# A decode step of attention plus GLU: TensorE's program rolled into a loop of seven turns over five heads, inside a hinted loop of two turns

## The chip, the core and the metric

The kernel runs on one core of a Trainium2 chip. The metric is device microseconds of one execution; the number given for the kernel before is the median of three runs. The profile is one execution, recorded by the hardware profiler.

## The reference

One decode step for a batch of two: a layer norm, then in parallel an attention over the last 2048 positions of a cache and a bilinear GLU, all added to the input. Everything is float32.

```python
B, D, Hq, Sk, Dh, F = 2, 512, 32, 8192, 128, 1376
xn = layernorm(x)                                  # x: [B, 1, D]
W = min(4096, max(256, Sk // 4))                   # 2048
q = (xn @ wq).reshape(B, 1, Hq, Dh)
k, v = k_cache[:, :, Sk - W:, :], v_cache[:, :, Sk - W:, :]     # [B, Hq, W, Dh]
p = softmax(einsum("bhqd,bhkd->bhqk", q, k) * Dh ** -0.5)
o = einsum("bhqk,bhkd->bhqd", p, v).reshape(B, 1, Hq * Dh)
h = (xn @ w_gate) * (xn @ w_up)
out = x + o @ wo + h @ w_down
```

Each head of each of the two sequences has its own keys and values, so each is used once: 134 MB of cache and 25 MB of weights are read for one result of 2 x 512.

## The kernel before, in words

The host lays all inputs out as one stream of blocks in the order in which the kernel needs them (`laid_out`, `blocks`). SyncE (SP) loads the blocks in that order into three slots of SBUF of 31 x 512 columns on 128 partitions; a load is issued when a slot is free, that is when every field of the block in it has been used (`pump`, `done`, lines 297 to 323). A head's keys are one field of 4096 columns: on each partition 16 positions of both sequences (line 746). Its values may be cut into pieces of 512 columns and spread over blocks (`vp` fields).

For each head, in order:

- `products`, `sums` (lines 432 to 443): VectorE (DVE) multiplies the keys by the query, which stands in PSUM, copied to all 128 partitions, and sums over the 128 elements of a position. Each is one instruction over 128 x 4096.
- `maxima`, `weights` (lines 445 to 466): DVE takes the largest score of each partition, GpSimd (POOL) the largest over the partitions, ScalarE (ACT) scales it and takes the exponentials, one instruction for each sequence, into p; POOL sums over the partitions, and DVE takes the reciprocal (`reciprocals`).
- `weigh` (line 484): TensorE (PE) multiplies p with the values, eight calls a head, into one of two banks `o_ps`. `copy_out` (line 494): ACT copies the bank to `o_sb`. `transpose` (line 501): PE brings the result to columns, ACT scales it into `oT`. `project_o` (line 520): PE multiplies by the head's part of `wo` and adds to `acc`.

The query projection is cut into a piece per head (`project_q`, two calls for each head into four heads' query in PSUM). The GLU is worked in the first blocks (`project_gu`, `gate`, `down`). The last heads are written out by hand (lines 659 to 720): for these, results are accumulated in a form spread over partitions (`accumulate`, four calls of 128 columns), and TensorE is given matmuls without use (`keep_busy`) between its steps.

All engines' instructions are recorded into one list in program order by `Flow.add` (line 162). `emit` (line 184) then finds which waits are needed and writes each engine's instructions, in the order of that list, with semaphore waits between the engines. So each engine runs strictly in the order of the program text, and all profile rows carry line 243, from which `emit` writes them; SP's waits are at line 242. A call of `pe.matmul` in float32 becomes two pairs of a weight load and a matmul.

Of the kernel before, what the change touches and what calls it, by code (L numbers as in the profile page):

```python
# [14 lines left out]
P = 128  # L15
B, D, H, DH, SK, F = 2, 512, 32, 128, 8192, 1376
W = min(4096, max(256, SK // 4))
J = W // P
# [6 lines left out]
LAG = 3  # L25
# [5 lines left out]
HG = 4  # L31
GC = HG * DH
JG = J // 4
CK, CQ, CO = B * J * DH, NC * GC, D
CP = CQ // NC
UNIT = CK + max(CP, CO)
STEP = 31 * FB
NP = 6
NV = CK // FB
KS = [3, 1, 2, 1, 2, 2, 1, 2, 2, 2, 1, 2, 2, 2, 1, 2, 2, 1]  # L40
WD = [(0, 2), (2, 4), (4, 7), (7, NFC - 1), (NFC - 1, NFC)]
NS = 3
BUFS = 3
BASE = 30 * 1024
FX = FR // NS

# [10 lines left out]
def blocks():  # L57

    def wd(n):
        return [("wd", i, D) for i in range(*WD[n])]

    def k(h):
        return [("k", h, CK)] + ([("wq", h, CP)] if h + HG < H else [])  # L70

    def v(h):
        return [("v", h, CK), ("wo", h, CO)]

    def gu(half):
        n = NC * (FH[half][1] - FH[half][0])
        return [("wg", half, n), ("wu", half, n)]

    ones = [("pick", 0, 8 * B), ("rows", 0, NFB * B)]
    first = [("x", 0, B * NC)] + ones + [("w", 0, NC * DH)]  # L80
    ahead = [[("w", 1, CQ - NC * DH)], gu(0) + gu(1), [("wr", 0, NS * P)] + wd(0)]
    pieces = [(h, n) for h in range(H - 1 - LAG) for n in range(NV + 1)]
    loads, h = [], 0
    for i, n in enumerate(KS):
        fields = (ahead[i] if i < len(ahead) else []) + sum((k(h + j) for j in range(n)), [])
        h += n
        room = (STEP - sum(w for _, _, w in fields)) // FB if i > 1 else 0
        taken, pieces = pieces[:room], pieces[room:]
        for g in sorted({g for g, _ in taken}):
            assert g < h - n  # L90
            ns = [m for t, m in taken if t == g]
            parts = [m for m in ns if m < NV]
            if parts:
                p0, p1 = parts[0], parts[-1] + 1
                fields.append(("vp", (g, p0, p1), FB * (p1 - p0)))
            if ns[-1] == NV:
                fields.append(("wo", g, CO))
        assert not pieces or pieces[0][0] >= h - NP
        loads.append(fields)
    assert not pieces and h == H - 1  # L100
    loads += [k(H - 1) + v(H - 1 - LAG) + wd(1)]
    out = [(("f", 0), first)] + [(("s", i), fields) for i, fields in enumerate(loads)]
    late, last = ("s", len(loads)), ("s", len(loads) + 1)
    out += [(late, v(H - 3)), (late, v(H - 2)), (last, [("v", H - 1, CK)])]
    out += [(last, [("wo", H - 1, CO)] + wd(2))]
    return out + [(last, wd(n)) for n in range(3, len(WD))]


class Flow:
# [7 lines left out]
    def __init__(self, nc):  # L117
        self.nc = nc
        self.units = {
            "pe": nc.tensor, "dve": nc.vector, "act": nc.scalar, "pl": nc.gpsimd, "sp": nc.sync,  # L120
        }
        self.ops, self.seen, self.free = [], {}, {}
        self.low = -(-nc.sbuf_base // 32) * 32
# [38 lines left out]
    def add(self, unit, make, writes, reads):  # L162
        n = len(self.ops)
        deps = set()
        for aps, write in ((reads, False), (writes, True)):
            for ap in aps:
                if not isinstance(ap.tensor, (bass.SBTensorHandle, bass.PSumTensorHandle)):
                    continue
                name, p0, p1, f0, f1 = self.box(ap)
                kept = []  # L170
                for old in self.seen.get(name, []):
                    m, w, a0, a1, b0, b1 = old
                    if m != n and (write or w) and a0 < p1 and p0 < a1 and b0 < f1 and f0 < b1:
                        deps.add((m, w))
                        if write and p0 <= a0 and a1 <= p1 and f0 <= b0 and b1 <= f1:
                            continue
                    kept.append(old)
                self.seen[name] = kept + [(n, write, p0, p1, f0, f1)]
        self.ops.append((unit, make, deps))
# [3 lines left out]

    def emit(self):
        nc, ops = self.nc, self.ops
        place, count = [], {}
        for n, (unit, make, deps) in enumerate(ops):
            key = ("dma", n) if make[0] == "dma_start" else unit
            count[key] = count.get(key, 0) + 1
            place.append((key, count[key]))  # L190
        knows = [None] * len(ops)
        known = {unit: {} for unit in self.units}
        waits = []
        for n, (unit, make, deps) in enumerate(ops):
            have = known[unit]
            need = {}
            for m, wrote in deps:
                key, at = place[m]
                if key == unit and (unit == "pe" or unit in ("dve", "act") and not wrote):
# [8 lines left out]
            ]  # L208
            for m in keep:
# [11 lines left out]
        told = {m for keep in waits for m in keep} | {len(ops) - 1}  # L221
        sems, value, at = {}, {}, {}
        order = sorted({place[m][0] for m in told}, key=lambda key: (key in ("dve", place[-1][0]), str(key)))
        if order[-1] != place[-1][0]:
            order.append(order.pop(-2))
        for key in order:
            sems[key] = nc.alloc_semaphore("done_" + (key if isinstance(key, str) else f"load{key[1]}"))
# [7 lines left out]
        for n, (unit, (method, args, kwargs), _) in enumerate(ops):  # L235
            eng = self.units[unit]
            keep = sorted(
                waits[n], key=lambda m: (isinstance(place[m][0], tuple) and m >= landed, m)
            )
            landed = max([landed] + [m for m in keep if isinstance(place[m][0], tuple)])  # L240
# [8 lines left out]
            if n == len(ops) - 2:  # L249
                assert unit == "dve"  # L250
                nc.vector.sem_clear(range(nums[0], nums[-2]))
        assert unit == "sp"
# [19 lines left out]
def sliding_attention_plus_glu_kernel(  # L272
# [13 lines left out]
    ]  # L286


    todo, at = [], 0
    for key, fields in blocks():  # L290
        todo.append((key, fields, at))
        at += P * pitch(fields)
    tiles, used, left, got = {}, {}, {}, {}
    for key, fields, _ in todo:
        left[key] = left.get(key, 0) + len(fields)

    def pump():
        while todo:
            key, fields, at = todo[0]
            if key not in tiles:  # L300
                if key[0] == "f":
                    n = sum(w for _, _, w in fields)
                    tiles[key] = flow.tile([P, n], "first")
                elif not slots:
                    return
                else:
                    tiles[key] = slots.pop(0)
                used[key] = 0
            todo.pop(0)
            c0 = used[key]  # L310
            for kind, i, w in fields:
                got[kind, i] = (tiles[key][:, used[key] : used[key] + w], key)
                used[key] += w
            c1 = used[key]
            src = stream[at : at + P * pitch(fields)].rearrange("(p i) -> p i", p=P)
            sp.dma_start(tiles[key][:, c0:c1], src[:, : c1 - c0])

    def done(kind, i):
        _, key = got.pop((kind, i))
        left[key] -= 1  # L320
        if left[key] == 0 and key[0] != "f":
            slots.append(tiles.pop(key))
            pump()

    pump()
    xT = got["x", 0][0].rearrange("p (b c) -> p b c", b=B)
    pick = got["pick", 0][0].rearrange("p (r s b) -> p r s b", s=2, b=B)
    rows = got["rows", 0][0]
# [22 lines left out]
    p_ring = [flow.tile([P, B, JG, 8 * B], f"p{i}") for i in range(NP)]  # L351
# [4 lines left out]
    oT_ring = [flow.tile([P, M], f"oT{i}") for i in range(4)]  # L356
    for t in oT_ring:
        pl.memset(t, 0.0)
# [21 lines left out]
    xnb = flow.tile([P, NC * B, P], "xnb")  # L380
    dve.tensor_copy(
        xnb, xn.rearrange("p c b -> p (c b)").unsqueeze(2).to_broadcast([P, NC * B, P])
    )

    q_ps, s_t, mm_t, p_t, sum_t, rec_t, o_sbs, oT = {}, {}, {}, {}, {}, {}, {}, {}
    n_acc = bank = 0

    q_banks = [flow.bank([P, B, GC], f"q{i}") for i in range(2)]

    def q_bank():  # L390
        q_banks.append(q_banks.pop(0))
        return q_banks[-1]

    def side(h):

        return int(h % 3 == 0)

    q_first = tr[:, P : 3 * P].rearrange("p (b n) -> p b n", b=B)

    def project_first(i):  # L400
        w = got["w", i][0].rearrange("p (c n) -> p c n", c=NC)
        if i == 0:
            q = q_first
        else:
            q_ps[0] = q_bank()
            q = q_ps[0][:, :, DH:]
        for b in range(B):
            for c in range(NC):
                pe.matmul(
                    q[:, b, :], xnb[:, c * B + b, :], w[:, c, :],  # L410
                    start=(c == 0), stop=(c == NC - 1),
# [410 lines left out]
```

## Time and profile before

| what | value |
|---|---|
| median of 3 runs | 376.09 us (375.97 to 376.46) |
| the profiled execution | span 374.6 us, from its first to its last instruction |
| instructions | 2741, of which 1094 matmuls and 1094 weight loads |
| busy | PE 66%, DVE 79%, ACT 16%, POOL 7% of the span |
| DMA | 159.70 MB, 426 GB/s over the span |
| packets of instructions | 8 of 16 KB on one queue, 4 of 8 KB on another |
| mean granted clock of TensorE | 0.813 |

Rows of the timeline read: start in us, length in us, engine, line, operation, output <- inputs, how many instructions were merged into the row, and in brackets the idle time before it with what ended it. Rows of the chain of waits read: start, length, what. The slices of the page cut the span in 40 parts of 9.37 us. "PEld" is TensorE's weight load, which overlaps its matmuls; "step" are the three slots.

### The profile page before, as it was taken

How to read it: one execution, taken by the hardware profiler on the slowest of the kernel's cores; microseconds unless marked ns; L12 is line 12 of the kernel's file. 1: busy time of each engine (PE TensorE's matmuls, PEld its weight loads, DVE VectorE, ACT ScalarE, POOL GpSimd, SP SyncE). 2: the span in 40 equal slices, each digit the busy share in tenths (PEclk: the TensorE clock that was granted, in tenths of full speed). 3: DMA queues.
4: the chain of work that ended last, by engine and by line, in shares of the span. 5: the costliest groups of instructions: out<-in, count | busy, mean ns of one | idle time of the engine just before them, and what ended most of it. 6: DMA issues, size and time to landing. Idle time of an engine off the chain costs nothing.

```text
span 374.6 us, 2741 instructions
## 1 busy us (share of the span) xinstructions
PE 248.4 (66%) x1094; PEld 86.8 (23%) x1094; DVE 295.1 (79%) x147; ACT 58.1 (16%) x259; POOL 25.3 (7%) x78
## 2 busy tenths in 40 slices
PE   3167675896578157855658585781488647476997
PEld 3033124231132013211212121320122112111344
DVE  3069998994599994599999945999999459999760
ACT  1002012111022012110202020300121201111232
POOL 1000000100001000000000000010001000000010
PEclk9759695898689758896969886998689868666999
DMA  8999999999999999999999999999999999999996
GB/s 345 420 465 454 450 432 435 434 434 424 427 427 434 434 434 434 436 434 441 434 435 429 434 434 434 434 429 434 434 435 434 429 434 434 428 426 416 414 432 250
DMA packets 3950, 159.70 MB, mean 426 GB/s; under 512 B 466, under 2 KB 610, under 8 KB 994
## 3 DMA queue, kind: packets, MB, share of 16 engines
q1 hardware_dynamic: 3938, 159.54, 98.6%
q8 instruction: 8, 0.13, 0.1%
q14 instruction: 4, 0.03, 0.0%
HBM read 159.47 MB, written 0.07 MB: 426 GB/s over the span
## 4 chain that ended last, share of the span: by engine, by line
DMA 64%; DVE 26%; PE 7%; ACT 1%; issue 0%; SPq 0%
DMA step<-in_stream_dram 64%; DVE s L243 13%; DVE step L243 13%; PE q L243 3%; PE acc L243 2%; PE o_ps L243 2%; PE tr L243 1%; ACT o_sb L243 0%; DVE m L243 0%; ACT oT L243 0%; DVE rec L243 0%; SPq L243 0%; DVE o_out L243 0%
## 5 line engine op out<-in xcount | busy, mean ns | idle before, releaser
L243 DVE TENSOR_TENSOR step<-step,q 128x4096 f32<-128x4096 f32 x31 | 136.8, 4411 | 47.0 <-DMA step<-in_stream_dram 47.0
L243 DVE TENSOR_REDUCE s<-step 128x32 f32<-128x4096 f32 x32 | 141.4, 4419 | 1.1
L243 PE MATMUL q<-step,xnb 128*128 128x512 f32 (+1 forms) x128 | 79.0, 759 | 80.5 <-DMA step<-in_stream_dram 80.5
L243 PE MATMUL o_ps<-step,p 128*16 128x512 f32 (+1 forms) x512 | 98.5, 730 | 11.2 <-DMA step<-in_stream_dram 11.2
L243 PEld LDWEIGHTS q<-step,xnb 128*128 128x128 f32 x128 | 28.0, 238 | 123.5 <-DMA step<-in_stream_dram 92.9
L243 PE MATMUL acc<-step,oT 128*9 128x512 f32 (+1 forms) x88 | 39.1, 604 | 8.7 <-ACT oT L243 8.7
L243 PE MATMUL tr<-first,o_sb 128*128 128x2 f32 (+2 forms) x198 | 29.1, 266 | 17.9 <-ACT o_sb L243 12.0
L243 PEld LDWEIGHTS tr<-first,o_sb 128*128 128x128 f32 x198 | 26.8, 205 | 40.6 <-ACT o_sb L243 31.3
L243 PEld LDWEIGHTS o_ps<-step,p 128*16 128x16 f32 x512 | 17.6, 107 | 78.6 <-issue 64.9
L243 ACT COPY o_sb<-o_ps 128x512 f32<-128x512 f32 (+1 forms) x24 | 13.8, 576 | 121.4 <-PE o_ps L243 121.4
L243 POOL PARTITION_ALL_REDUCE mm<-m x32 | 11.3, 355 | 268.6 <-DVE m L243 258.7
L243 ACT ACTIVATE nm<-mm 128x2 f32<-128x2 f32 x32 | 6.5, 203 | 148.0 <-POOL mm L243 148.0
L243 ACT ACTIVATE p<-s,nm 128x16 f32<-128x16 f32 x64 | 19.2, 300 | 1.0
L243 POOL PARTITION_ALL_REDUCE sum<-rs x32 | 12.7, 398 | 69.1 <-ACT p L243 69.1
L243 ACT ACTIVATE oT<-tr,rec 128x1 f32<-128x1 f32 x64 | 12.2, 260 | 27.0 <-PE tr L243 27.0
L243 DVE TENSOR_TENSOR step<-step,tr 128x4096 f32<-128x4096 f32 x1 | 4.4, 4422 | 14.8 <-DMA step<-in_stream_dram 14.8
L243 ACT ACTIVATION_READ_ACCUMULATOR p<-s,nm 128x1 f32 x64 | 11.9, 187 | 0.0
L243 PE MATMUL o_ps<-step,xn 128*2 128x512 f32 (+1 forms) x48 | 10.1, 548 | 0.0
L243 PEld LDWEIGHTS acc<-step,oT 128*9 128x9 f32 x88 | 4.6, 94 | 21.1 <-ACT oT L243 14.5
L243 DVE TENSOR_TENSOR o_out<-acc,x_nat 128x128 f32<-128x128 f32 x1 | 0.3, 292 | 8.4 <-PE acc L243 8.4
L243 DVE TENSOR_REDUCE m<-s 128x2 f32<-128x32 f32 x32 | 6.0, 186 | 1.1
L243 DVE RECIPROCAL rec<-sum 128x2 f32<-128x2 f32 x32 | 5.0, 155 | 1.9 <-POOL sum L243 1.9
(43 smaller groups left out, 41.5 us busy)
## 6 DMA issues: line engine op xcount, KB each, us to landing
step<-in_stream_dram SPq DMA_DIRECT2D x14, 7936.0 KB, 37.7
step<-in_stream_dram SPq DMA_DIRECT2D x2, 7680.0 KB, 32.0
step<-in_stream_dram SPq DMA_DIRECT2D x1, 7872.0 KB, 58.2
step<-in_stream_dram SPq DMA_DIRECT2D x1, 7808.0 KB, 38.8
step<-in_stream_dram SPq DMA_DIRECT2D x1, 4864.0 KB, 30.3
step<-in_stream_dram SPq DMA_DIRECT2D x2, 2304.0 KB, 19.6
step<-in_stream_dram SPq DMA_DIRECT2D x1, 2048.0 KB, 18.3
step<-in_stream_dram SPq DMA_DIRECT2D x1, 1024.0 KB, 19.8
```

Source lines behind the costliest of these rows:

```text
L243: made = getattr(eng, method)(*args, **kwargs)
```

## The change

TensorE's program is no longer written out head by head. The heads after the first three are taken in six turns of five, T = 6, G = 5; a seventh turn runs one of the sections alone. The body is written once, and for that every turn must address the same places, so the layout is made periodic:

- The keys and values of a head are laid out with one sequence on each half of the partitions (PB = 64), 32 positions each, still 128 x 4096. The query of a head is one row that differs between the halves; `project_q` makes the queries of five heads at once (eight calls, into PSUM) and ACT copies them to SBUF (`q_sb`). The maximum is taken by two DVE instructions, one on each half.
- A block has a fixed slot, and a slot may be loaded in part: a load is issued when the columns that it overwrites are no longer live. A turn has three blocks, with the keys of two, two and one heads, and the values of the five heads that are three behind.
- p, `oT`, `rec` and others are rings of five. The results of heads 0 and 1 of a turn share one bank (`SPLIT`), those of heads 2, 3 and 4 the other.
- PE's waits inside the loop are on token semaphores that hold the same value in each turn: another engine adds a token when its work is done, PE takes it off. A load's landing is told by SP, which waits for it (`tell`) and then adds the token.
- Of the GLU's last product two chunks stay early, one (`HOLE`) is moved behind the loop, its weights in a gap of the last query weights, and seven are accumulated at the end. `keep_busy` is gone.

The loop itself, and the loop of two turns around all of TensorE's program:

```python
TWICE = ("pe",)

    @contextlib.contextmanager
    def twice(self, unit):
        if unit not in TWICE:
            yield
            return
        eng = self.units[unit]
        with self.nc.Fori(0, 2, engines=(eng.engine,), hint_back_edge=True) as turn:
            with eng.If(turn > 0):
                yield
...
            # in emit, for PE: body has sections "q", "a", "b"; turns is 6, 7, 6
            with nc.tensor.Fori(0, max(turns.values())) as turn:
                for section, ns in body.items():
                    short = turns[section] < max(turns.values())
                    with nc.tensor.If(turn < turns[section]) if short else contextlib.nullcontext():
                        for n in ns:
                            write(n)
...
            if part:
                for key in sorted(points[part[0], part[2]]):
                    eng.wait_ge(sems["token", key], 1).then_inc(sems["token", key], -1)
```

The blocks of the stream (slot, first column, fields), with `vp(h, p0, p1)` a part of a head's values:

```python
    out.append((1, 0, k(*range(AHEAD))))                       # AHEAD = 3
    out.append((2, 0, [("wq", 0, CQ)] + gu + [("wr", 0, NS * P)] + wd(range(NE))))
    k0, v0 = AHEAD, 0
    for t in range(T):
        last = t == T - 1
        out.append((0, 0, k(k0, k0 + 1) + vp(v0) + vp(v0 + 1, 0, VA)))        # VA = 5
        out.append((1, 0, k(k0 + 2, k0 + 3) + vp(v0 + 1, VA) + vp(v0 + 2) + vp(v0 + 3, 0, VB)))
        b, c = vp(v0 + 3, VB), vp(v0 + 4)                                     # VB = 1
        if not last:
            out.append((2, 0, [("wq", t + 1, CQ)] + k(k0 + 4) + b + c))
        else:
            at = CQ + CK
            out += [(2, at, b), (2, at + sum(w for _, _, w in b), c)]
        k0, v0 = k0 + G, v0 + G
    # then: values of head 30, of head 31 in two parts, wo of 31 with four chunks
    # of w_down, two chunks, one chunk
```

And the order of the program, which is each engine's order:

```python
    def part_a(t):
        with flow.loop("a", t):
            weigh(G * t, 0, NV)
            weigh(G * t + 1, 0, VA)

    def post(t, group):
        d = transpose(group, copy_out(group))
        scale_out(group, d)
        for n in SPLIT[group]:
            project_o(G * t + n)

    def part_b(t):
        with flow.loop("b", t):
            weigh(G * t + 1, VA, NV)
            post(t, 0)
            weigh(G * t + 2, 0, NV)
            weigh(G * t + 3, 0, VB)

    def part_c(t):
        with flow.loop("b", t):
            weigh(G * t + 3, VB, NV)
            weigh(G * t + 4, 0, NV)
            post(t, 1)

    for t in range(T):
        part_q(t)
        h = AHEAD + G * t
        scores(h, lambda: part_a(t))         # scores: products, sums, then(),
        scores(h + 1)                        #         maxima, weights, reciprocals
        scores(h + 2, lambda: part_b(t))
        scores(h + 3)
        if h + 4 < H:
            scores(h + 4, lambda: part_c(t))
        else:
            reciprocals(h + 3)
            part_c(t)
    part_a(T)

    down(HOLE)
    acc_sb = flow.tile([M, D], "acc_sb")
    dve.tensor_copy(acc_sb, acc)
    weigh(H - 1, VA, NV)
    o_sb = copy_out(0)
    accumulate(carry, acc_sb)
    d = transpose(0, o_sb)
    n = len(SPLIT[0])
    dve.tensor_tensor(oT[:, :n, ::RB], d, rec[:, :n, :], op=ALU.mult)
    chunks = [c for group in TAIL for c in group]
    for c in chunks[:3]:
        down(c)
    project_o(H - 2)
    project_o(H - 1)
    for c in chunks[3:]:
        down(c)
```

More of the change, by code (lines that the diff above doesn't have):

```diff
@@ L1 @@
+import contextlib
 import math
@@ L57, in blocks @@
 def blocks():
[L66 to L106, printed above, removed]
+    def k(*heads):
+        return [("k", h, CK) for h in heads]
+    def vp(h, p0=0, p1=NV):
+        return [("vp", (h, p0, p1), FB * (p1 - p0))] + ([("wo", h, CO)] if p1 == NV else [])
@@ L394, in side @@
[L394 to L408, printed above, removed]
+    xnb = xnb.rearrange("p (c b) n -> p c (b n)", b=B)
+    s_t, mm_t, sum_t = {}, {}, {}
+    q_ps = flow.bank([P, 4 * FB // 2], "q")
@@ L479, in accumulate, with weigh @@
         n_acc += 1
-    def keep_busy(n):
-        pe.matmul(spare[:, 0:n], mean_w, spare_in[:, 0:n], start=True, stop=True)
-    def weigh(h, v, parts, first, last):
-        for n, part in enumerate(parts):
-            b, i = divmod(part, JG)
+    def weigh(h, p0, p1):
+        group = next(n for n, g in enumerate(SPLIT) if h % G in g)
+        heads = SPLIT[group]
+        v = got["vp", (h, p0, p1)]
+        cols = 4 * B * len(heads)
+        for n in range(p0, p1):
+            k, i = divmod(n, 4)
@@ L675, in sliding_attention_plus_glu_kernel, with scores @@
-    transpose([H - 6, H - 5], o_sbs[1])
-    for g in (H - 7, H - 6, H - 5):
-        project_o(g)
-    keep_busy(256)
-    maxima(h)
-    reciprocals(h - 1)
-    products(h + 1)
-    o_sb = pv([HF])
-    down(1)
+    def scores(h, then=None):
+        products(h)
+        sums(h)
+        if then:
+            then()
+        maxima(h)
+        weights(h)
+        if h >= 1:
+            reciprocals(h - 1)
+    project_first()
+    for h in range(AHEAD):
+        scores(h)
+    for half in range(2):
+        project_gu(half)
@@ new lines, in sliding_attention_plus_glu_kernel, with part_q @@
+    gate()
+    for c in range(NE):
+        down(c)
+    down_rest()
+    def part_q(t):
+        with flow.loop("q", t):
+            project_q(t)
+    def part_a(t):
[13 more added lines that the diff above has]
+            weigh(G * t + 3, 0, VB)
```

546 lines of the change are left out of this document (279 added, 267 removed).

## The prediction

> **What bounds the kernel now.** I read the page first: span, slices, queues.
>
> ```profile
> span 374.6 us, 2741 instructions
> PE 248.4 (66%) x1094; PEld 86.8 (23%) x1094; DVE 295.1 (79%) x147; ACT 58.1 (16%) x259; POOL 25.3 (7%) x78
> DMA  8999999999999999999999999999999999999996
> GB/s 345 420 465 454 450 432 435 434 434 424 427 427 434 434 434 434 436 434 441 434 435 429 434 434 434 434 429 434 434 435 434 429 434 434 428 426 416 414 432 250
> q1 hardware_dynamic: 3938, 159.54, 98.6%
> q8 instruction: 8, 0.13, 0.1%
> DMA 64%; DVE 26%; PE 7%; ACT 1%; issue 0%; SPq 0%
> step<-in_stream_dram SPq DMA_DIRECT2D x14, 7936.0 KB, 37.7
> ```
>
> The 16 DMA engines are full from the first slice to the last, at 434 GB/s, and 159.5 MB must come in: the body of the kernel is the stream. A block of 7,936 KB needs 18.7 us of that rate and lands 37.7 us after its issue, so a whole block still stands ahead of it in the queue when it is issued: the releases of the buffers have that much to spare. Only the head and the tail can move the time, and whatever slows the stream itself. Then the chain of waits, its last pieces, and the timeline of the last 20 us:
>
> ```profile
> 340.49 0.19 DVE m L243
> 340.68 0.07 DVE rec L243
> 340.75 4.33 DVE step L243
> 345.08 0.02 issue
> 345.10 4.43 DVE s L243
> 349.53 0.02 issue
> 349.55 18.29 DMA step<-in_stream_dram
> 367.84 0.04 issue
> 367.89 1.06 PE o_ps L243 x16
> ```
>
> ```profile
> 21.98 4.42 DVE L243 TENSOR_TENSOR step<-step,tr 128x4096 f32<-128x4096 f32 x1 [14.81 <-DMA step<-in_stream_dram]
> ...
> 352.07 4.42 DVE L243 TENSOR_TENSOR step<-step,q 128x4096 f32<-128x4096 f32 x1 [2.26 <-DMA step<-in_stream_dram]
> ...
> 357.01 4.40 DVE L243 TENSOR_REDUCE s<-step 128x32 f32<-128x4096 f32 x1
> ...
> 361.44 0.19 DVE L243 TENSOR_REDUCE m<-s 128x2 f32<-128x32 f32 x1
> ...
> 361.72 0.35 POOL L243 PARTITION_ALL_REDUCE mm<-m  x1 [2.62 <-DVE rec L243]
> ...
> 362.70 0.29 ACT L243 ACTIVATE p<-s,nm 128x16 f32<-128x16 f32 x1
> ...
> 372.26 0.12 PEld L243 LDWEIGHTS acc<-step,hT 128*9 128x9 f32 x8 [0.22 <-DMA step<-in_stream_dram]
> 372.74 0.29 DVE L243 TENSOR_TENSOR o_out<-acc,x_nat 128x128 f32<-128x128 f32 x1 [8.38 <-PE acc L243]
> 373.05 0.35 SPq L243 DMA_DIRECT2D out_dram<-o_out  x1
> ```
>
> The last load lands at 372.2, TensorE ends at 372.7, 0.5 us behind it, and the output takes 1.9 more to 374.6. The last head's keys land at 352.07 (20 us ahead of the stream's end), its sums end at 361.4, its weights p are ready at 363.0, and TensorE then waits for values until 367.8. So the softmax of the last head has 4.8 us to spare. This tail is what the change rebuilds. The time shown, 376.09, is 1.5 us above the profiled span of 374.6; I work on the span and add that 1.5 at the end. About 0.2% (0.75 us) can be told from no change.
>
> **The change, part by part.** *Bytes.* Caches and weights are the same; only the order and the placing in the three slots differ. Blocks of 30x512 columns (7,864 KB decimal, 18.1 us at 434 GB/s) follow one another: per turn two blocks with two heads' keys each and one with a single head's keys. Nothing for the sum.
>
> *DVE.* Products and sums keep their shape (128x4096), so a head costs what the chain shows from one m (340.49) to the point after the next sums (349.55): 9.06 us. The maximum becomes two reduces on half the partitions, at most another 0.19. Five heads take 46 us of a turn of 54.4: hidden behind the stream, with 8 us to spare per turn. The releases: slot 0 of the next turn needs the projection of the turn's first two heads (second block's landing plus some 6 us), slot 1 that of the third head (third block's landing plus some 11 us), both due 18 us after those landings, when the block ahead has landed. I price mid-stream gaps at nothing; if a release came 8 us later than this, they would cost what is over.
>
> *TensorE's program.* What a loop can save is the fetching of its instructions: 8 packets, 0.13 MB, so 16 KB each. At 0.1% of 16 engines' 374.6 us they hold 6 us of engine time (3 to 9 by the rounding), 0.4 to 1.1 each, and a load ends with its slowest engine. If the loop fetches nothing, the stream ends between 0 and 1.1 us earlier; I take 0.4, since fetches at the start and end stay and the other engines' do too. The two-turn wrapper costs a jump over the program and back, before the first load has landed: nothing, unless it takes longer than the 15 us that DVE waits for the first keys.
>
> *Tokens.* SP now also waits on a load and then tells TensorE, so its DMA issues queue behind these waits; in program order each issue needs consumers of the same or a later load, so none is held back by one. Nothing, to some tenths of a us per hand-over.
>
> *The tail.* This is the term that counts. In the sixth turn the keys of heads 30 and 31 lie in the second block. Call its landing B. Behind it come 2,097 + 2,359 + 2,359 + 1,311 + 786 + 1,311 + 524 + 262 KB = 11.01 MB, 25.4 us at 434 GB/s. The stream's end, 372.2 less 0.4 = 371.8, puts B at 346.4. From there, in us after B:
>
> DVE still owes 0.3 of the block before (two heads, 18.4 with the additional maxima, against 18.1 per block), then two heads: sums of head 31 end at 18.6. From sums to p took 361.41 to 362.99 before, 1.6: p of head 31 is ready at 20.2, 5.2 ahead of the stream's end; before it was 9.2 ahead.
>
> What stands behind it is the point. The sixth turn has no fifth head, so `part_c(5)` is written after `scores(31)`. ScalarE runs in program order: its copy of the bank for heads 27 to 29 stands behind the exponentials of head 31, which wait for DVE until 18.8. TensorE has the values of 28 and 29 at 4.8 and 10.3 and is through with them at 12, then stands at the transposes until the copy comes, and everything later stands behind: three projections, then all of heads 30 and 31. The rows that price it:
>
> ```profile
> 340.61 6.37 PE L243 MATMUL o_ps<-step,p 128*16 128x512 f32 x38 [5.31 <-DMA step<-in_stream_dram]
> ...
> 344.00 0.17 PEld L243 LDWEIGHTS o_ps<-step,p 128*16 128x16 f32 x4 [0.68 <-issue]
> ...
> 345.10 0.11 PEld L243 LDWEIGHTS o_ps<-step,p 128*16 128x16 f32 x4 [0.32 <-issue]
> ...
> 349.45 2.74 PE L243 MATMUL acc<-step,oT 128*9 128x512 f32 x6
> ...
> 358.07 1.90 PE L243 MATMUL o_ps<-step,p 128*16 128x512 f32 x16
> ...
> 360.04 0.59 ACT L243 COPY o_sb<-o_ps 128x512 f32<-128x512 f32 x1 [1.43 <-PE o_ps L243]
> 360.68 1.05 PEld L243 LDWEIGHTS tr<-first,o_sb 128*128 128x128 f32 x8 [0.48 <-ACT o_sb L243]
> ...
> 361.85 0.41 ACT L243 ACTIVATE oT<-tr,rec 128x1 f32<-128x1 f32 x2 [1.23 <-PE tr L243]
> ...
> 370.83 0.84 PE L243 MATMUL acc<-step,hT 128*9 128x128 f32 x24
> ```
>
> ```profile
> 135.15 3.78 PE q L243 x4
> ```
>
> ```profile
> 3.76 0.58 PE L243 MATMUL tr<-st,mean_w 128*128 128x2 f32 x2 [3.76 <-DVE st L243]
> ```
>
> The two weight-load rows show how the pace changes: four loads every 0.85 us (0.17 busy, 0.68 idle) up to 344.0, every 0.43 from 345.1, so TensorE needs some 4 us of work after its pause to come up to speed.
>
> Step by step, fast end and slow end: copy 0.65 (20.8); transposes, 8 instructions, 1.1 (or 2.3 at the 0.29 each that the first matmuls show) to 21.9 or 23.1; the first scaled pair 0.45; three projections, 6 instructions, 2.7 (or 4.6, at 0.95 each as in the q row until TensorE has run for some 4 us) to 25.1 or 28.2; weighing head 30, 16 instructions, 1.9; the first five pieces of head 31, 1.2; leaving the loop, of which no row of this trace has a price, 0.2, taken from short gaps between instructions and bounded by 0 and by 2 us for a fetch (below); the moved chunk in 512 columns, 2 instructions at 0.46, 0.9; three pieces, 0.7; copy with its hand-overs 0.8; transposes 1.1; three accumulations (24 instructions) 0.84, two projections 0.56, four accumulations 1.1. Sum: 34.4 or 37.4. TensorE ends at 346.4 + 34.4 = 380.8 or 383.8, that is 9 to 12 behind the last landing where it was 0.5. The idle stretch from 12 to 20.8 is longer than the 5.31 in the row above, after which 38 instructions took 6.37 (0.17 each) where 16 in a dense stretch took 1.90 (0.12 each), so the chain's start is slow; its later part is dense. I take 36.0: TensorE ends at 382.4, the span at 384.3, the time at 385.8.
>
> [...]
>
> **Rivals.** [...]
>
> [...]
>
> *Faster by the fetches alone.* Place: the last landing. If ScalarE's order does not hold TensorE, since head 31's scores are there early, only the slowest DMA engine counts: it ends up to 1.1 earlier, 375.0 to 376.0. It decides from the point where p of head 31 stands 14 us ahead of the stream's end; by the rows it is 5.2. Against it is that DVE needs 18.4 us for two heads that land 25.4 ahead of the end.
>
> *In between.* The copy gets past (an order other than I read), but p at 20.2 still leads: five pieces 1.2 or 2.1, 0.2, 0.9, 0.7, 0.8, 1.1, 2.5: 27.6 to 29.5, TensorE ends 374.0 to 375.9, the time 377.4 to 379.3.
>
> **How the numbers follow.** Tail chain as worked out 0.66 (384.2 to 387.2 between its ends); with more fetching 0.16 (388.5 to 391); in between 0.08; faster 0.07; a remainder of 0.03 within 0.2%. All but the last two are slower: 0.90, same 0.03, faster 0.07. The range takes the first case whole and nearly all of the second, and reaches below the first for hand-overs mis-sized by 2 us or more: 381.5 to 390.5. Left out are the faster, same and in-between cases (0.18) and the far end of the second (0.02).
>
> **What would show it.** In the profile after: the last stream landing within 1 us of 372.2; the last k landing near 346 and the last sums ending near 365; then on ScalarE the copy of the bank right behind the last exponentials; TensorE idle for some 8 us ahead of the transposes of heads 27 to 29; the chain ending in PE and ACT pieces of 14 to 17 us, and DMA slices that fall to nothing about 12 us before the span's end. [...] I am wrong if DMA is busy up to the last 3 us, or if mid-stream slices fall below 420 GB/s.

## The result, and the profile after

The changed kernel takes 408.9 us (median of 4 runs, 407.92 to 409.72) against 376.05 us before (375.97 to 376.46): 1.0869 times as long, with an interval of 1.0851 to 1.0887. It is slower, as predicted, but by 32.9 us where 9.7 were forecast, and 18 us beyond the range. The page of the changed kernel, cut to the lines that answer to those of before, with one group of instructions (columns: count, busy time, mean ns of one, idle time ahead of them with its releaser):

```profile
span 408.4 us, 2613 instructions
...
DMA  8998999985999999999989999999999999996491
GB/s 365 426 464 386 475 392 475 391 385 193 428 421 398 463 403 373 397 404 463 409 367 433 409 409 457 409 367 445 380 427 451 403 397 403 415 403 292 186 415 49
...
q1 hardware_dynamic: 4226, 159.54, 92.5%
q8 instruction: 2, 0.03, 0.0%
...
L330 POOL PARTITION_ALL_REDUCE mm<-m x32 | 109.9, 3434 | 227.5 <-DVE m L330 227.5
```

The same bytes came in, but the stream no longer runs through. Slice 10 moved 193 GB/s, slices 37 and 38 292 and 186, and the middle averages less than the 434 of before. TensorE's instruction packets fell from 8 to 2. The line that nobody asked for is the last one. GpSimd's maximum over the partitions is the same instruction as before, on the same operands, and the group of before has it at a tenth of the time:

```profile
L243 POOL PARTITION_ALL_REDUCE mm<-m x32 | 11.3, 355 | 268.6 <-DVE m L243 258.7 <-DVE rec L243 9.9
```

VectorE's waits in the changed kernel (columns: waited for, total us, times, longest) say that the stream is not what it waits for. Before, its one large wait was the landing of keys, 61.9 us in 17 times. Now:

```profile
DVE step L330 <- ACT q_sb L330: 35.8, 3, 15.5
DVE step L330 <- ACT first L330: 29.8, 3, 10.5
DVE step L330 <- DMA step<-in_stream_dram: 10.2, 1, 10.2
```

`q_sb` and `first` are the two buffers into which ScalarE copies the queries of a turn. So once in each of the six turns the products wait for their queries. The timeline of the changed kernel shows one whole turn of that, with the start of the first turn ahead of it (start, length, engine, instruction, idle time before it; "SPq" is SyncE's queue, and its row here is the load of the second turn's first block):

```profile
67.20 4.43 DVE L330 TENSOR_TENSOR step<-step,q_sb 128x4096 f32<-128x4096 f32 x1 [15.54 <-ACT q_sb L330]
...
96.94 0.33 SPq L330 DMA_DIRECT2D step<-in_stream_dram  x1
...
181.84 4.43 DVE L330 TENSOR_TENSOR step<-step,q_sb 128x4096 f32<-128x4096 f32 x1 [10.24 <-ACT q_sb L330]
...
219.37 4.64 POOL L330 PARTITION_ALL_REDUCE mm<-m  x1 [3.15 <-DVE m L330]
219.39 4.41 DVE L330 TENSOR_TENSOR step<-step,q_sb 128x4096 f32<-128x4096 f32 x1
224.04 0.20 ACT L330 ACTIVATE nm<-mm 128x2 f32<-128x2 f32 x1 [8.31 <-POOL mm L330]
225.13 0.58 ACT L330 COPY o_sb<-o_ps 128x512 f32<-128x512 f32 x1
225.86 1.84 PE L330 MATMUL tr<-first,o_sb 128*128 128x6 f32 x8 [6.94 <-PEq L322]
228.30 4.18 PE L330 MATMUL acc<-step,oT 128*9 128x512 f32 x6 [0.59 <-PEq L322]
228.75 0.35 POOL L330 PARTITION_ALL_REDUCE mm<-m  x1 [3.15 <-DVE m L330]
232.41 4.59 PE L330 MATMUL q<-step,xnb 128*128 128x512 f32 x16
237.03 0.69 ACT L330 COPY first<-q 128x640 f32<-128x640 f32 x1 [6.83 <-PE q L330]
237.83 4.43 DVE L330 TENSOR_TENSOR step<-step,first 128x4096 f32<-128x4096 f32 x1 [8.97 <-ACT first L330]
...
352.30 4.42 DVE L330 TENSOR_TENSOR step<-step,first 128x4096 f32<-128x4096 f32 x1 [10.46 <-ACT first L330]
```

Two things are to be read here. First, the all-reduce at 219.37 starts with the fifth head's product and ends with it (223.8 and 224.0). The one at 228.75 has no product beside it and takes 0.35. Secondly, the rows close a ring. VectorE takes four heads (37.5 us from 181.84 to 219.37), GpSimd's maximum of the fourth stands beside the fifth product (4.7), ScalarE takes the exponentials (1.1) and only then, in its order, copies the bank (0.7); TensorE transposes (2.4 with ScalarE's scaling), projects three heads (4.1) and makes the next turn's queries (4.6); ScalarE copies these (0.8); and VectorE may begin the next turn. The sum is 56.0, which is 237.83 less 181.84. From the first turn's product at 67.20 to the sixth's at 352.30 there are five turns of 57.0 us on average; the one shown is the shortest. The stream needs 54.4 for a turn, so the ring sets the pace, slots come free late, and the stream dries. All of TensorE's idle time that this leaves is put down to its sequencer (PEq), which stands at a token: over the run 62.6 us ahead of the weighings, 100.3 ahead of the transposes, 7.1 ahead of the projections. TensorE's pace enters the ring too: its granted clock is 0.50 from 221 to 231 us, and its transposes and projections, 6.6 us here, take 4.2 in the tail, where it is 1.00; by these rows the low clock is worth some 2.3 us of the ring, an estimate that no run tested.

The first standstill comes before the ring has closed once. The first turn's queries are made behind the products of the GLU, so its first product began at 67.20, although its keys had landed at 56.3. The load of the second turn's first block waits for results of this turn; it was issued at 96.94, when the block ahead of it had landed at 92.7, and the stream stood still from 92.4 to 97.9 us (slice 10). No run made these first queries earlier.

The tail of the changed kernel, in the same columns, has the order that the prediction described:

```profile
387.12 3.63 PE L330 MATMUL o_ps<-step,p 128*24 128x512 f32 x30 [0.21 <-PEq L322]
...
390.88 0.32 ACT L330 ACTIVATE p<-s,nm 64x32 f32<-64x32 f32 x1
...
391.31 0.58 ACT L330 COPY o_sb<-o_ps 128x512 f32<-128x512 f32 x1
...
392.04 1.03 PE L330 MATMUL tr<-first,o_sb 128*128 128x6 f32 x8 [1.29 <-PEq L322]
...
403.87 1.06 PE L330 MATMUL acc<-step,hT 128*9 128x128 f32 x32
```

ScalarE's copy stands right behind the last exponentials, and TensorE ends 13.7 us after them. But here the order costs little: the bank itself is full only at 390.75, half a microsecond before the exponentials end, and TensorE stands for 1.29 us ahead of its transposes, where some 8 were forecast.

### The profile page after: what moved, and what is told of

It reads as the page before. It is cut to its first block, busy times and chain, and to the rows that moved or that the text cites. A ratio compares the mean times of both kernels' runs of the same rounds, so it can differ in the third digit from the quotient of the medians.

```text
span 408.4 us, 2613 instructions
## 1 busy us (share of the span) xinstructions
PE 200.2 (49%) x940; PEld 73.6 (18%) x940; DVE 302.5 (74%) x179; ACT 59.5 (15%) x250; POOL 124.2 (30%) x84
## 5 line engine op out<-in xcount | busy, mean ns | idle before, releaser
L330 POOL PARTITION_ALL_REDUCE mm<-m x32 | 109.9, 3434 | 227.5 <-DVE m L330 227.5
L330 PE MATMUL o_ps<-step,p 128*24 128x512 f32 (+1 forms) x512 | 82.3, 670 | 62.6 <-PEq L322 62.6
L330 DVE TENSOR_TENSOR step<-step,q_sb 128x4096 f32<-128x4096 f32 x15 | 66.1, 4409 | 35.8 <-ACT q_sb L330 35.8
L330 DVE TENSOR_TENSOR step<-step,first 128x4096 f32<-128x4096 f32 x14 | 61.7, 4409 | 29.8 <-ACT first L330 29.8
L330 PE MATMUL tr<-first,o_sb 128*128 128x6 f32 (+1 forms) x118 | 25.8, 337 | 102.6 <-PEq L322 100.3
L330 PEld LDWEIGHTS o_ps<-step,p 128*24 128x24 f32 (+1 forms) x512 | 19.0, 104 | 110.1 <-issue 108.1
L330 PE MATMUL q<-step,xnb 128*128 128x512 f32 (+1 forms) x96 | 28.1, 446 | 0.0
L330 ACT ACTIVATE p<-s,nm 64x32 f32<-64x32 f32 x64 | 20.4, 319 | 1.4
L330 PEld LDWEIGHTS q<-step,xnb 128*128 128x128 f32 x96 | 15.3, 195 | 19.3 <-issue 19.3
L330 DVE TENSOR_REDUCE m<-s 64x1 f32<-64x32 f32 x64 | 11.5, 180 | 1.5
L330 ACT ACTIVATION_READ_ACCUMULATOR p<-s,nm 64x1 f32 x64 | 11.8, 185 | 0.0
L330 PEld LDWEIGHTS o_ps<-step,xn 128*2 128x2 f32 x48 | 2.8, 95 | 32.9 <-DMA step<-in_stream_dram 23.6
## 6 DMA issues: line engine op xcount, KB each, us to landing
step<-in_stream_dram SPq DMA_DIRECT2D x17, 7680.0 KB, 23.8
```

The source lines that it names most:

```text
L330: made = getattr(eng, method)(*args, **kwargs)
```

## The experiments

The theory after the result: GpSimd's maximum is held up while VectorE multiplies two operands from SBUF (4.64 us beside the product at 219.39, 0.35 at 228.75); that makes the ring longer than a turn of the stream; the tail order costs what was predicted; the wrapper costs little. The rival: the loop's branches refetch instructions, or the wrapper's hint does, and TensorE is late for that reason. Times are medians, each beside runs of the kernel before on the same chip (376.04, 376.29 and 375.99 in the three groups of runs).

### Queries read from PSUM

```diff
-        act.copy(q_sb[t % 2], q_ps[:, :GC])
...
-        q = ... q_sb[t % 2][:, n * DH : (n + 1) * DH]
+        q = ... q_ps[:, n * DH : (n + 1) * DH]
```

> The queries are read from PSUM by the products, as before, and the copy to SBUF is gone; nothing else differs. Theory (the all-reduce of GpSimd is held up while VectorE multiplies two SBUF operands, and its 4.64 us lie on a ring VectorE - GpSimd - ScalarE - TensorE - VectorE that closes once per turn): the all-reduce of m is back at 0.35 us in every head, a turn goes from 57.0 to the stream's 54.4 us or the ring's 52, the profile loses 20 us or more: 384 to 390 us. Rival (the loop itself, its branches, tokens and a TensorE that is cold sets the turn): the turn stays at 56 to 57 us, the time within 3 us of 408.9.

Measured: 392.09 us (390.92 to 392.93), 1.0431 times before (1.0414 to 1.0448), 16.8 below the changed kernel and just above the 384 to 390 expected. The group of the all-reduce, and then the first products of the first, second and sixth turn with three rows of the tail, from the timeline:

```profile
L330 POOL PARTITION_ALL_REDUCE mm<-m x32 | 11.3, 354 | 305.0 <-DVE m L330 305.0
```

```profile
65.85 4.42 DVE L330 TENSOR_TENSOR step<-step,q 128x4096 f32<-128x4096 f32 x1 [14.38 <-PE q L330]
...
116.59 4.42 DVE L330 TENSOR_TENSOR step<-step,q 128x4096 f32<-128x4096 f32 x1 [3.65 <-PE q L330]
...
331.25 4.42 DVE L330 TENSOR_TENSOR step<-step,q 128x4096 f32<-128x4096 f32 x1 [7.29 <-DMA step<-in_stream_dram]
...
369.81 0.32 ACT L330 ACTIVATE p<-s,nm 64x32 f32<-64x32 f32 x1
...
370.97 1.84 PE L330 MATMUL tr<-first,o_sb 128*128 128x6 f32 x8 [5.25 <-PEq L322]
...
385.48 1.06 PE L330 MATMUL acc<-step,hT 128*9 128x128 f32 x32
```

All 32 maxima are back at 0.35 us. The first turn takes 50.7 us: the 56.0 of the ring less the 4.3 by which the maximum was held up and the 0.8 of the copy would be 50.9. Once the first turns have caught up, VectorE waits for landings again. The sixth turn's first product starts 21.05 us earlier than in the changed kernel, and the span ends 18.8 earlier; the tail's chain is 2.7 longer (370.13 to 386.54, 16.4 us instead of 13.7). TensorE had stood for 5.25 us, and its eight transposes take 1.84 instead of the 1.03 after a pause of 1.29; the granted clock is 0.50 from 371 to 377 us here, and 1.00 from 388 to 395 there.

### No outer loop, and no hint

```diff
-TWICE = ("pe",)
+TWICE = ()
```

> The outer loop of two turns and its hint are taken away; the inner loop stays. If the hint keeps the inner loop's code in place: 14 to 21 packets of instructions in place of 2, each turn longer by 1 to 4 us since TensorE lies on the ring, 415 to 430 us. Rival (the code stays in place without it, the wrapper does nothing but delay TensorE's start): 2 to 4 packets, 408 to 409 us, the first matmul 1.5 us earlier.

Measured: 406.23 us (405.48 to 407.62), 1.0812 times before (1.0791 to 1.0833), with 2 packets of instructions, as in the changed kernel. This is below both expectations. The loop's code stays in place without wrapper or hint, and the rival falls. What the wrapper costs is 2.7 us. TensorE's first matmul comes later with it; the first row is of the changed kernel, the second of this one, from their timelines:

```profile
7.22 0.57 PE L330 MATMUL tr<-st,mean_w 128*128 128x2 f32 x2 [7.22 <-issue]
```

```profile
5.42 0.59 PE L330 MATMUL tr<-st,mean_w 128*128 128x2 f32 x2 [5.42 <-DVE st L330]
...
64.97 4.43 DVE L330 TENSOR_TENSOR step<-step,q_sb 128x4096 f32<-128x4096 f32 x1 [14.44 <-ACT q_sb L330]
```

The 1.8 us reach the first turn (64.97 instead of 67.20), and the ring hands them on. The rest is at the end: the output takes 3.0 us to land with the wrapper, 1.6 without (the row with it is below). With the loop kept and its hint alone taken out:

```diff
-        with self.nc.Fori(0, 2, engines=(eng.engine,), hint_back_edge=True) as turn:
+        with self.nc.Fori(0, 2, engines=(eng.engine,), hint_back_edge=False) as turn:
```

> The kernel after, its outer loop of two turns kept, the hint for its closing branch taken away. If the hint decides where the second packet of instructions falls: the packet at 406 us, beside the output, goes to another time and the output lands 1.4 us earlier, 407 to 407.8 us. Rival (the empty turn alone does it): 2 packets at 4 and 406 us and 408.9 as it was.

Measured: 407.62 us (407.12 to 408.89), 1.0844 times before (1.0828 to 1.086). The trace has the two packets at 3.4 and 10.5 us here, at 4.1 and 406.0 in the changed kernel, and at 59.3 and 397.0 without the outer loop. The output's issue (KB, us to landing), in the changed kernel and in the one without hint:

```profile
out_dram<-o_out SPq DMA_DIRECT2D x1, 64.0 KB, 3.0
```

```profile
out_dram<-o_out SPq DMA_DIRECT2D x1, 64.0 KB, 1.5
```

So in this pair the hint's one effect that can be seen is that a packet is fetched when the loop closes, beside the output, which lands 1.5 us later. That the hint always does this is not shown: four of the kernels below have it and fetch a single packet, at 4 us. The medians differ by 1.3 us (the intervals of the two ratios overlap slightly). Over all kernels here it holds: three have a packet in their last microseconds, and their outputs land in 2.6, 3.0 and 3.4 us; in the others, with hint or without, the output takes 1.5 or 1.6.

### Queries made a turn earlier, still in SBUF

```diff
+    project_q(0)
     for t in range(T):
-        part_q(t)
...
-            scores(h + 4, lambda: part_c(t))
+            scores(h + 4, lambda: (part_q(t + 1), part_c(t)))
```

> The queries of the next turn are projected right after the third block lands, ahead of the results of heads 2 to 4, so that the products of the next turn no longer wait for these results; queries stay in SBUF. Theory of the ring: the all-reduce stays at 4.64 us, but no longer matters; VectorE needs 47 us a turn, the turn comes down to the stream's 54.4: 384 to 393 us. Rival (the slow all-reduce costs by itself wherever it lies, or TensorE is the bound): over 400 us.

Measured: 395.39 us (394.43 to 396.32), 1.0519 times before (1.0492 to 1.0545). The groups and VectorE's waits:

```profile
L330 POOL PARTITION_ALL_REDUCE mm<-m x32 | 105.6, 3301 | 207.6 <-DVE m L330 207.6
```

```profile
DVE step L330 <- DMA step<-in_stream_dram: 44.3, 7, 10.2
DVE step L330 <- ACT q_sb L330: 14.5, 1, 14.5
```

Here the maximum is left held up (3.30 us on average) and only the ring is opened. VectorE waits for landings again, and 13.5 us are gained. The 14.5 us are the first turn's wait for its queries, and the stream still stands still there, for 4.4 us at 92 us. So in the later turns the held-up maximum costs its time through the ring; where nothing waits for p, 4.3 us more for it are cheap. It lies slightly above the 384 to 393 expected.

### The tail's order

With the queries early, the last turn's `part_c` was put ahead of the last head's exponentials:

```diff
-        scores(h + 3)
+        scores(h + 3, None if h + 4 < H else lambda: part_c(t))
         if h + 4 < H:
...
         else:
             reciprocals(h + 3)
-            part_c(t)
```

> As the one with early queries, and in the last turn the results of heads 27 to 29 are copied out ahead of the exponentials of head 31 on ScalarE. Theory of the tail as predicted (what stands behind the last p is 13.6 us in the profile after, of which copy, transposes, projections and the weighing of head 30 are 6 to 8): 6 to 8 us less than the one with early queries, 377 to 386 us. Rival (the last landing or VectorE's sums set the end by then): under 3 us less.

Measured: 394.27 us (393.68 to 395.3), 1.049 times before (1.0469 to 1.0512): 1.1 us less than without it, where 6 to 8 were expected. This missed. Three rows of its timeline:

```profile
373.55 0.35 POOL L330 PARTITION_ALL_REDUCE mm<-m  x1 [3.15 <-DVE m L330]
...
373.86 0.58 ACT L330 COPY o_sb<-o_ps 128x512 f32<-128x512 f32 x1 [3.95 <-PE o_ps L330]
...
376.54 0.23 ACT L330 ACTIVATE nm<-mm 128x2 f32<-128x2 f32 x1
```

The values of heads 28 and 29 came so late that TensorE was through with them only at 373.8. ScalarE, in order, waited for them, and now the last exponentials stood behind the copy: the maximum was there at 373.9, and its scaling came at 376.5. The order is a gain only where the bank is full before the last maximum.

The same edit on the kernel with the queries in PSUM:

> Queries read from PSUM and projected at the turn's start as in the kernel after, the results of heads 27 to 29 copied out ahead of the last exponentials. If the order of the tail is worth the 5.8 us that it made between the two kernels with early queries: 385 to 388 us, against 392.1 with queries from PSUM alone. Rival (it was worth that only because VectorE was late there): over 390.

Measured: 383.62 us (383.23 to 386.52), 1.0228 times before (1.0188 to 1.0268): 8.5 us less than with the queries in PSUM alone, where 4 to 7 were expected. Here the copy comes at 366.3 us, well ahead of the last exponentials. And without the outer loop as well:

> The same without the outer loop and its hint. If the late start of TensorE is hidden where the stream sets the pace and only the packet beside the output counts: 1 to 2 us less than the same with the outer loop. Rival (packets in the stream cost as much): within 0.5 us of it.

Measured: 382.23 us (381.5 to 382.7), 1.0167 times before (1.015 to 1.0184). It is the best version that was found, and still 6.2 us (1.7%) slower than before. Where the stream ends is shown by a table of single microseconds (first busy shares of PE, PEld, DVE, ACT and POOL, each with a count; then granted clock, DMA's busy share, GB/s), of this kernel and of the one before:

```profile
376.00:377.00 1.00, 1.00 (x32) 0.98 (x35) 0.16 (x1) 0.00 (x0) 0.00 (x0) 1.00 0.02 8
377.00:378.00 1.00, 1.00 (x48) 1.00 (x40) 0.00 (x0) 0.00 (x0) 0.00 (x0) 1.00 0.00 0
```

```profile
371.00:372.00 1.00, 1.00 (x44) 0.96 (x40) 0.00 (x0) 0.36 (x2) 0.00 (x0) 1.00 0.31 121
372.00:373.00 1.00, 0.67 (x21) 0.16 (x12) 0.27 (x1) 0.00 (x0) 0.00 (x0) 1.00 0.00 0
```

The last load lands 4.5 us later than before (376.7 instead of 372.2), and TensorE ends 5.8 us later (378.5 instead of 372.7). Two loads account for the 4.5. The second turn's second block landed 20.8 us behind the one ahead of it instead of 18.1, since it was issued only 2.9 us before that one landed; it waits for results of the first turn, whose first product again began late (64.12, its keys landed at 55.6). The values of head 30 landed 7.4 us behind the load ahead of them instead of 5.4, issued again 2.9 us before it landed. And the tail's last part:

```profile
369.73 0.32 ACT L330 ACTIVATE p<-s,nm 64x32 f32<-64x32 f32 x1
...
374.34 0.59 ACT L330 COPY o_sb<-o_ps 128x512 f32<-128x512 f32 x1 [4.21 <-PE acc L330]
...
377.41 1.06 PE L330 MATMUL acc<-step,hT 128*9 128x128 f32 x32
```

p of the last head is ready at 370.05, 7.1 us later than before (363.0), and 8.4 us of TensorE's work follow. But TensorE does not wait for this p: from 367.20 to 374.23, with the projections of heads 27 to 29 and the weighing of heads 30 and 31, its rows show no idle time. So in this kernel the late keys of heads 30 and 31, which lie in one block, are not shown to set the end; it is TensorE's own row of work. No kernel with these keys placed earlier was tried.

### Both remedies at once

Queries in PSUM, made a turn earlier, and the tail's order:

> All three edits together: queries read from PSUM, next turn's queries projected early, results of heads 27 to 29 copied out ahead of the last exponentials. If the ring, the slow all-reduce and the tail's order are separate causes, the all-reduce is at 0.35, the turn at 54.4, and TensorE does the projections of 27 to 29 while VectorE still sums: 382 to 387 us, 5 to 9 less than with queries from PSUM alone. Rival (the tail is a row of TensorE's own work, whatever the order): 389 to 392.

Measured: 410.09 us (408.27 to 411.47), 1.0886 times before (1.0861 to 1.0912). This was a plain miss. Two rows of its timeline:

```profile
220.06 2.04 PE L330 MATMUL q<-step,xnb 128*128 128x512 f32 x2 [5.46 <-PEq L322]
...
225.31 6.07 PE L330 MATMUL q<-step,xnb 128*128 128x128 f32 x14 [3.21 <-PEq L322]
```

There is one bank of queries. Made early, the next turn's queries must wait until the fifth head's product has read the old ones, and TensorE stands there with everything behind it, `part_c` and so the releases. The stream then stood still for 11.3 us at 112 us. Without the outer loop:

> The same without the outer loop and its hint. If the wrapper's price is a late start on the ring and a packet of instructions beside the output, the late start is now hidden behind the stream and the output's 1.5 us stay: 1 to 2 us less than with the wrapper. Rival (a packet in the middle of the stream costs as much as it saves): within 0.5 us.

Measured: 408.34 us (406.92 to 412.42), 1.0886 times before (1.0841 to 1.0932); this cannot be told from the one with the loop. With the tail as in the change:

> Queries from PSUM and projected early, the tail in the order of the kernel after. Against the one with all three it prices the order of the tail alone: 5 to 8 us more if ScalarE's order holds TensorE as predicted, under 2 if not. Against queries from PSUM alone it prices the early projection, 0 to 2 us, since the turn was at the stream's pace there from the third on.

Measured: 415.86 us (415.56 to 416.64), 1.1059 times before (1.1043 to 1.1075): the tail's order is worth 5.8 us here. The early projection, against the queries in PSUM alone, costs 23.8 us where 0 to 2 were expected.

A second bank would take that wait away. Queries made early and copied by ScalarE, as in the change, but into PSUM; with the tail's order and no outer loop:

```diff
+    q_two = flow.bank([P, 4 * FB // 2], "q_two")
...
-        act.copy(q_sb[t % 2], q_ps[:, :GC])
+        act.copy(q_two[:, :GC], q_ps[:, :GC])
```

> Queries projected early and copied by ScalarE from their bank into a second bank of PSUM, from which the products read; tail as in the two others; no outer loop. The all-reduce stays at 0.35 us, since no operand but the keys is in SBUF, and neither VectorE nor TensorE waits for the other's bank: the turn is at 54.4 from the second on, 381 to 386 us. Rival (ScalarE's copy, which waits for the fifth product, holds the results behind it): 386 to 395.

Measured: 388.97 us (386.67 to 391.07), 1.0324 times before (1.0283 to 1.0365). The time lies outside the 381 to 386 expected and inside the rival's range, and the rows of the first turn show the rival:

```profile
108.56 0.68 ACT L330 COPY q_two<-q 128x640 f32<-128x640 f32 x1 [3.06 <-DVE step L330]
109.26 0.59 ACT L330 COPY o_sb<-o_ps 128x512 f32<-128x512 f32 x1
...
109.99 1.84 PE L330 MATMUL tr<-first,o_sb 128*128 128x6 f32 x8 [5.36 <-PEq L322]
```

ScalarE's copy of the queries waits until VectorE's fifth product has read the old ones, the copy of the results stands behind it, and TensorE waits for that. The next block was issued at 114.3, and the stream stood still for 2.4 us at 113 us. The group of the all-reduce answers the other question:

```profile
L330 POOL PARTITION_ALL_REDUCE mm<-m x32 | 11.3, 354 | 298.2 <-DVE m L330 298.2
```

With the copy kept and only its place moved from SBUF to PSUM, the maximum takes 0.35 us, against 3.30 on average with early queries in SBUF. It is the second operand's place, and not the copy, that holds GpSimd up.

## Why the prediction was wrong, point by point

**Where the 32.9 us went.** One path through the runs gives it: 408.90 to 392.09 with the queries in PSUM (16.8: held-up maximum, copy and ring together), to 383.62 with the tail's order (8.5), to 382.23 without the outer loop (1.4), and 6.2 left over the 376.05 of before. In another order the parts are others: behind early queries in SBUF, the tail's order was worth 1.1.

**The step that failed** is the one on the releases: "I price mid-stream gaps at nothing; if a release came 8 us later than this, they would cost what is over." It had compared VectorE's 46 us for five heads with a turn of 54.4 and found 8 us to spare. It checked the releases only against the landings, as if TensorE's results came a fixed time behind each. But a turn's queries are made behind the results of the turn before, which wait for ScalarE's copy, which stands behind the fourth head's exponentials. The prediction saw this very order, of the copy behind the exponentials, and priced it in the sixth turn alone. In the first five turns the same order closes a ring of 50.7 us even with the maximum at 0.35 (the first turn with the queries in PSUM), 3.7 and not 8 us short of the stream's. The copy of the queries was in the change's description and was not priced either.

In the prediction's own terms: it had the two releases some 6 and 11 us behind the landings of the second and third block. With the queries in PSUM they came 7.4 and 10.7 behind (third turn, issues at 193.6 and 215.0), much as it said. In turns two to five of the changed kernel they came 14.6 to 16.3 and 15.1 to 16.6 behind, and in the first turn, whose late queries the prediction did not look at, 22.6 and 22.8. Nor was a release in time up to the moment when the block ahead landed: the load issued at 154.3, 2.0 us before that moment, landed 21.4 us after it instead of 18.1. So the last load came 28 us late (400.1 instead of 371.8): 7.2 of these arose in the first turn, 11.5 in the four behind it, 9.4 in the last.

**The held-up maximum** took these 3.7 us and more. No row of before shows it, since there the query lay in PSUM. The rows of the runs do: 0.35 us becomes 4.64 beside a product of 4.41 with both inputs in SBUF, and is 0.35 again with one input in PSUM. How the one instruction holds the other they do not show; the all-reduce's record starts 0.02 us ahead of the product's. The price is 4.3 us on the way to p.

**The tail** was right as a mechanism, but in the changed kernel it hardly acted. With the ring out of the way (queries in PSUM), the chain behind the last p took 16.4 us, where the prediction had 15.8, between 14.2 and 17.2, and TensorE ended 10.9 us behind the last landing, where it had 9 to 12. Taking the order away was worth 8.5 and 5.8, against the 7.4 between its forecast and its in-between case (36.0 less some 28.6). In the changed kernel the values came so late that the order held the copy up by half a microsecond; TensorE ended 4.9 us behind the last landing, and that the chain of 13.7 lies near the forecast is in part luck. And with the queries in PSUM p itself came later than worked out: 370.1 and not 366.6. Of these 3.5 us, 2.9 stand already in the sixth turn's first product, at 331.25 where the stream was to have delivered at 328.3 (two blocks had landed 19.7 and 19.5 us behind the ones ahead of them at the first turn's late releases, instead of 18.1); a head took 9.38 us and not up to 9.25, which makes up the rest over four heads. So even this kernel is 6.3 us above 385.8.

**Instruction packets.** That the loop saves fetches was right: 2 packets were seen where there had been 8. Their gain, taken at 0.4, could not be seen apart from the rest. The case with more fetching (388.5 to 391) fell with one or two packets in every version of the loop. With seven turns there were at most 2 packets in all, hinted or not, so no fetch per turn took place. No run shows the 2 us for a fetch that stands as a bound in the sum of the tail, nor a price behind 388.5 to 391: in the changed kernel TensorE is busy throughout from 394 to 400 us, where it leaves the loop, and its two packets, at 4.1 and 406.0 us, lie outside the chain of the tail.

**The wrapper**, priced at nothing, cost 1.4 to 2.7 us. The prediction looked at the wait for the first keys; but it is the first turn's queries that hang on TensorE's start.

**The other rivals.** The faster one fell: TensorE's work, and not the last landing, set the end. The in-between case is what the best version came near to: from p on it took 8.4 us, as worked out there (7.4 to 9.3), with p 3.4 us late; but since TensorE did not wait for that p, the agreement is in part luck. The sign that the prediction gave for being wrong, slices in mid-stream below 420 GB/s, is the one that came.

**What stays open.** The last 6.2 us are split by the rows, not by a run: 4.5 belong to a stream that ends later, by the two loads named above, and most of the rest to TensorE, which ends 1.8 us behind the last landing instead of 0.5. Whether earlier queries in the first turn would win the larger part back was not tried. What the hand-overs by tokens cost was not measured by itself.

## What to carry to other kernels

When a kernel is turned into a loop, write down the ring that leads from one turn's first instruction to the next turn's, through every engine's own order, and compare its sum with the turn of whatever bounds the kernel: slack counted per engine says nothing of it. Price the first turn by itself: what it waits for is something else. An operand that is moved from PSUM to SBUF is a change for the other engines too (0.35 us became 4.64 here); look at what GpSimd runs beside that instruction. And when an order is found that hurts in the last turn, ask what it does in all the others.

## What was not expected of the hardware

- GpSimd's all-reduce over the partitions takes 0.35 us by itself and 4.64 beside a VectorE product whose two inputs lie in SBUF; with one of them in PSUM it stays at 0.35.
- A loop of seven turns on TensorE kept its code: one or two packets of instructions for the whole run, with or without a hint or an outer loop. The straight program before took 8.
- One packet of instructions fetched beside the closing output of 64 KB went with a landing in 2.6 to 3.4 us (three kernels) instead of 1.5 or 1.6.
- A loop whose first turn is empty delayed TensorE's first matmul from 5.42 to 7.22 us (6.51 without the hint). With the best order it cost 1.4 us of the time (383.62 against 382.23).
